# Emitting each engine's instructions straight into the main body instead of inside a Block

## The chip, the cores and the metric

The kernel runs on one core of a Trainium2 chip. The metric is the device time of one execution in microseconds (us). The profile covers a *span*, from the first to the last instruction that it records; the time is 1.3 to 1.9 us longer than the span, and that remainder will matter. Engines are called as in the profile: PE is TensorE (PEld its weight loads), DVE is VectorE, ACT is ScalarE, POOL is GpSimd, SP is SyncE. A "q" after an engine's name means its sequencer.

## The reference

```python
x  = A_x                                   # 1 x 2048 x 512, bf16
xn = layernorm(x)
h[t] = Lam_bar * h[t-1] + (xn @ B_bar.T)[t]           # complex state, 512 wide
A  = 2 * Re(h @ C.T) + xn * Dskip
B  = (gelu(xn @ w_gate) * (xn @ w_up)) @ w_down       # 512 -> 1376 -> 512
out = x + A + B
```

What is computed does not matter here: the change leaves every operation, its order and its waits alone.

## The kernel before

The kernel records its operations, schedules them and then emits one program per engine. An operation waits on semaphores for what it needs and raises one when it is done. The emission is the part that is changed:

```python
        final_waits = [(op.sem, 16) for op in sorted(self.out_ops, key=lambda o: o.finish)]
        block = es.enter_context(nc.Block())

        def body_for(ename):
            prog = plan[ename]

            def body(h):
                for waits, op in prog:
                    for (s, v) in waits:
                        h.wait_ge(s, v)
                    ins = op.fn(h)
                    ins.then_inc(op.sem, 1 if op.kind == "eng" else 16)
                if ename == "sync":
                    for (s, v) in final_waits:      # 17 stores of the output
                        h.wait_ge(s, v)
            return body

        for e in ENGINES:
            if plan[e] or e == "sync":
                {"tensor": block.tensor, "vector": block.vector, "scalar": block.scalar,
                 "gpsimd": block.gpsimd, "sync": block.sync}[e](body_for(e))
```

`nc.Block()` gives each engine a body of its own. In the program that is built from it, the main body ends with one unconditional branch per engine (the entry branch), each engine's body ends with another to the Block's end, and there stands an all-engine barrier: every engine drains (the drain of PE lasts 1.2 us in the records and ends at 174.18 us, 0.05 us after the last matmul) and raises a "gather" semaphore, POOL waits for the other four and raises a "release" semaphore, and every engine waits for that. The records of its line hold the five drains and six semaphore instructions, two of them on POOL and one on each other engine. A barrier of the same form stands at the start of the program (its last records are at 0.66 to 0.72 us), behind POOL's MEMSETs of the constants; it is not part of the Block and stays.

The last lines of the work itself are these. DVE adds the last part of a tile and SP stores it:

```python
                V(lambda e: e.tensor_tensor(OUTB[ko].ap[:, c0:c1], PS[bank][:, c0:c1], XD[tt].ap[:, c0:c1], ALU.add), ...)
                S.dma(lambda e: e.dma_start(out[0, 128 * tt:128 * (tt + 1), c0:c1], OUTB[ko].ap[:, c0:c1]), ...,
                      is_output=True, tag="st_out")
```

Of the kernel before, what the change touches and what calls it, by code (L numbers as in the profile page):

```python
# [77 lines left out]
class Sched:  # L78
# [212 lines left out]
    def emit(self):  # L291
        nc, es = self.nc, self.es
        order = self.order
        esem = {}
        for e in ENGINES:
            if any(op.kind == "eng" for op in order[e]):
                esem[e] = es.enter_context(nc.semaphore("q_" + e))
        cnt = {e: 0 for e in ENGINES}
        nd = 0
        for e in ENGINES:  # L300
            for op in order[e]:
                if op.kind == "eng":
                    cnt[e] += 1
                    op.sem, op.val = esem[e], cnt[e]
                else:
                    op.sem, op.val = es.enter_context(nc.semaphore("d%d" % nd)), 16
                    nd += 1
        self.n_sems = len(esem) + nd
        plan = {}
        nwait = 0  # L310
        for e in ENGINES:
            seen = {}
            prog = []
            for op in order[e]:
                need = {}
                for d in op.deps:
                    if d.kind == "eng" and d.eng == e and (e == "tensor" or d is op.behind):
                        continue
                    key = ("e", d.eng) if d.kind == "eng" else ("d", d.id)
                    if seen.get(key, 0) >= d.val:  # L320
                        continue
                    if key not in need or need[key].val < d.val:
                        need[key] = d
                for key, d in need.items():
                    seen[key] = d.val
                waits = [(d.sem, d.val) for d in need.values()]
                nwait += len(waits)
                prog.append((waits, op))
            plan[e] = prog
        self.n_waits = nwait  # L330
        final_waits = [(op.sem, 16) for op in sorted(self.out_ops, key=lambda o: o.finish)]
        block = es.enter_context(nc.Block())

        def body_for(ename):
            prog = plan[ename]

            def body(h):
                for waits, op in prog:
                    for (s, v) in waits:
                        h.wait_ge(s, v)  # L340
                    ins = op.fn(h)
                    ins.then_inc(op.sem, 1 if op.kind == "eng" else 16)
                if ename == "sync":
                    for (s, v) in final_waits:
                        h.wait_ge(s, v)
            return body

        for e in ENGINES:
            if plan[e] or e == "sync":
                {"tensor": block.tensor, "vector": block.vector, "scalar": block.scalar,  # L350
                 "gpsimd": block.gpsimd, "sync": block.sync}[e](body_for(e))


L, D, P, F = 2048, 512, 512, 1376
# [720 lines left out]
```

## Time and profile before

| | |
|---|---|
| time, median of the first 3 runs | 178.57 us (178.27 to 178.67) |
| profiled execution: time, span | 178.19 us, 176.6 us |
| PE busy | 98% of the span |
| first load and first weight load start | 0.74 and 0.75 us |
| last DVE addition ends, last store is issued | 174.46 and 174.49 us |
| span ends | 176.65 us |

The page of the profile: its first lines, and from its part 4 the chain of work that ended last.

```profile
span 176.6 us, 2515 instructions
## 1 busy us (share of the span) xinstructions
PE 173.4 (98%) x891; PEld 84.9 (48%) x891; DVE 162.4 (92%) x283; ACT 90.3 (51%) x169; POOL 10.3 (6%) x25
...
## 4 chain that ended last, share of the span: by engine, by line
PE 98%; DVE 0%; issue 0%
```

TensorE bounds the body. Nothing that the change removes stands between two matmuls, so only the start and the end can move.

The timeline of the start (start us, duration us, engine, line, operation):

```profile
0.34 0.10 POOL L1060 MEMSET const-uint8-127<- 128x1 uint8 x1
0.74 0.41 SPq L498 DMA_DIRECT2D arena<-in_A_x_dram  x1
0.74 1.28 ACT L480 ACT_TABLE_LOAD   x1 [0.74 <-PEq L1060]
0.75 0.14 PEld L913 LDWEIGHTS PS<-const-bfloat16-1.0 128*128 128x128 bf16 x2 [0.75 <-issue]
```

L1060 is the line that makes the program object; its MEMSETs and the opening barrier carry that number. Between 0.44 us, when the MEMSETs end, and 0.74 us lies the opening barrier, which stays.

The records of the closing barrier's line, L374 (engine, instruction, count: shortest, median, longest in ns, first and last start in us):

```profile
L374 POOLq EVENT_SEMAPHORE  x2: 17/17/17, 176.2 to 176.3; - x2
...
L374 PEldq DRAIN  x1: 1200/1200/1200, 173.0 to 173.0; - x1
...
L374 SPq COMPARE_BRANCH  x1: 33/33/33, 176.0 to 176.0; - x1
L374 SPq DRAIN  x1: 7/7/7, 176.2 to 176.2; - x1
L374 ACTq EVENT_SEMAPHORE  x1: 17/17/17, 176.3 to 176.3; - x1
...
L374 PEldq EVENT_SEMAPHORE  x1: 51/51/51, 176.3 to 176.3; - x1
L374 SPq EVENT_SEMAPHORE  x1: 17/17/17, 176.6 to 176.6; - x1
```

Read it as a chain. SP's branch at 176.0 carries the last of the 17 waits for stores. SP drains and raises the gather; POOL gathers and releases (176.2, 176.3); PE, DVE and ACT pass at 176.3. SP passes last, at 176.6, and with that the span ends. To the nanosecond, from the same records: SP's last paired wait ends at 175.972, its branch stands at 176.038, its drain at 176.177, POOL's release at 176.288, PE's pass at 176.342 and SP's at 176.630.

### The profile page before, as it was taken

Reading aid. Unit: us, or ns where it says so; the run is one execution under the profiler, and the core shown is the slowest. Engines: PE = TensorE matmul, PEld = TensorE weight load, DVE = VectorE, ACT = ScalarE, POOL = GpSimd, SP = SyncE. Lnnn points to the kernel's source line nnn. Section 1 sums busy time; section 2 is a strip of 40 time slices with the busy share of each in tenths; the row PEclk is TensorE's granted clock in tenths of the full one; section 3 lists DMA queues with packets and bytes.
Section 4 is the critical chain, followed back from the end, with each engine's and each line's share of the span. In section 5 each row is a group of like instructions: output and inputs, shape, how many; then the busy total and the mean of one; then the engine's idle time right before and its main releaser. Section 6 shows DMA issues by size and latency. Waiting matters only on the chain.

```text
span 176.6 us, 2515 instructions
## 1 busy us (share of the span) xinstructions
PE 173.4 (98%) x891; PEld 84.9 (48%) x891; DVE 162.4 (92%) x283; ACT 90.3 (51%) x169; POOL 10.3 (6%) x25
## 2 busy tenths in 40 slices
PE   8999999999999999999999999999999999999994
PEld 3954464444544444444644444444454444444453
DVE  6989999987999999889999999999999999999961
ACT  4575568899866898003676792000767780000000
POOL 3212040220000000020000000000000000000000
PEclk9999999999999999999999999999999999999999
DMA  5997999984999000011024000002001000000131
GB/s 156 322 318 162 184 212 158 111 156 89 218 302 185 4 0 2 0 59 59 4 57 92 2 0 0 4 7 82 30 8 21 4 0 0 0 0 0 64 132 46
DMA packets 33396, 14.36 MB, mean 81 GB/s; under 512 B 23688, under 2 KB 33384, under 8 KB 33384
## 3 DMA queue, kind: packets, MB, share of 16 engines
q1 hardware_dynamic: 32944, 13.87, 35.1%
q10 hardware_dynamic: 440, 0.33, 0.6%
q8 instruction: 7, 0.11, 0.3%
q14 instruction: 5, 0.04, 0.1%
HBM read 6.46 MB, written 2.10 MB: 48 GB/s over the span
## 4 chain that ended last, share of the span: by engine, by line
PE 98%; DVE 0%; issue 0%
PE PS L864 37%; PE PS L823 32%; PE PS L734 16%; PE PS L698 7%; PE PS L797 3%; PE PS L913 2%; PE PS L673 1%; PE PS L920 0%; DVE arena L882 0%
## 5 line engine op out<-in xcount | busy, mean ns | idle before, releaser
L864 PE MATMUL PS<-arena 128*128 128x512 bf16 (+3 forms) x323 | 66.2, 367 | 0.0
L823 PE MATMUL PS<-arena 128*128 128x512 bf16 x264 | 58.1, 379 | 0.0
L864 PEld LDWEIGHTS PS<-arena 128*128 128x128 bf16 (+1 forms) x323 | 30.8, 98 | 35.2
L823 PEld LDWEIGHTS PS<-arena 128*128 128x128 bf16 x264 | 25.8, 98 | 30.4
L767 DVE TENSOR_TENSOR_SCAN arena<-arena 128x512 bf16<-128x512 f32 x32 | 38.8, 1253 | 0.0
L838 ACT ACTIVATE arena<-PS 128x512 bf16<-128x512 f32 x33 | 19.8, 599 | 37.0 <-PE PS L823 34.5
L734 PE MATMUL PS<-arena 128*128 128x512 bf16 x128 | 28.1, 379 | 0.0
L842 ACT ACTIVATE arena<-PS 128x512 bf16<-128x512 f32 x33 | 19.7, 597 | 4.7 <-PE PS L823 4.5
L856 ACT ACTIVATE PS<-arena 128x512 f32<-128x512 bf16 (+2 forms) x17 | 9.6, 581 | 20.4 <-PE PS L864 19.7
L734 PEld LDWEIGHTS PS<-arena 128*128 128x128 bf16 x128 | 12.5, 98 | 14.9
L738 ACT ACTIVATE arena<-PS 128x512 bf16<-128x512 f32 x32 | 17.7, 595 | 2.3 <-PE PS L734 2.3
L882 DVE TENSOR_TENSOR arena<-PS,arena 128x512 bf16<-128x512 f32 (+2 forms) x17 | 10.8, 652 | 5.0 <-PE PS L864 4.5
L844 DVE TENSOR_TENSOR arena<-arena 128x512 bf16<-128x512 bf16 x33 | 13.0, 416 | 1.7 <-ACT arena L842 1.4
L698 PE MATMUL PS<-arena 128*128 128x192 bf16 (+2 forms) x80 | 13.1, 320 | 0.0
L624 DVE BATCH_NORM_STATS2 arena<-arena 128x6 f32<-128x512 bf16 x16 | 10.3, 682 | 0.9 <-DMA arena<-in_A_x_dram 0.9
L754 DVE TENSOR_TENSOR arena<-arena 128x4096 bf16<-128x4096 bf16 (+1 forms) x5 | 9.2, 1860 | 0.5 <-ACT arena L619 0.5
L698 PEld LDWEIGHTS PS<-arena 128*128 128x128 bf16 x80 | 7.4, 100 | 4.7 <-issue 0.2
L756 DVE TENSOR_TENSOR arena<-arena 128x4096 bf16<-128x4096 bf16 (+1 forms) x5 | 9.2, 1860 | 0.4 <-ACT arena L620 0.4
L707 ACT ACTIVATE arena<-PS,arena 128x192 bf16<-128x192 f32 (+1 forms) x16 | 6.7, 447 | 4.9 <-PE PS L698 4.1
L779 DVE TENSOR_TENSOR arena<-arena 128x4096 bf16<-128x4096 bf16 x4 | 9.2, 2289 | 0.1
L780 DVE TENSOR_TENSOR arena<-arena 128x4096 bf16<-128x4096 bf16 x4 | 9.1, 2285 | 0.0
L710 DVE SCALAR_TENSOR_TENSOR arena<-PS,arena 128x192 bf16<-128x192 f32 (+1 forms) x16 | 6.6, 444 | 0.7 <-ACT arena L707 0.7
(84 smaller groups left out, 111.1 us busy)
## 6 DMA issues: line engine op xcount, KB each, us to landing
out_dram<-arena SPq DMA_DIRECT2D x15, 128.0 KB, 1.7
arena<-in_A_x_dram SPq DMA_DIRECT2D x3, 512.0 KB, 5.3
arena<-in_B_w_down_dram SPq DMA_DIRECT2D x1, 1280.0 KB, 8.4
arena<-in_B_w_gate_dram SPq DMA_DIRECT2D x2, 256.0 KB, 5.2
arena<-in_B_w_up_dram SPq DMA_DIRECT2D x2, 256.0 KB, 5.4
arena<-in_B_w_gate_dram SPq DMA_DIRECT2D x1, 480.0 KB, 5.8
arena<-in_B_w_up_dram SPq DMA_DIRECT2D x1, 480.0 KB, 5.9
arena<-arena SPq DMA_TRANSPOSE x25, 2.6
```

The lines of the kernel that those rows point to most:

```text
L624: return (V(lambda e: e.bn_stats(ST[tt].ap, X[tt].ap), d_dve_1x(512), [X[tt]], [ST[tt]], "bnst"), V(lambda e: e.bn_aggr(MVt[b][j].ap, ST[t ...
L698: ins_ = e.matmul(dst, XCd(j, k), WGU[:, us[0]:us[-1] + 1, k, f0:f1], start=(k == 0), stop=(k == KD - 1))
L734: ins_ = e.matmul(PS[bank][:, :], BBT[c][dk].ap[:, 128 * s:128 * (s + 1)], XNT[b].ap[:, dk, :], start=(dk == 0), stop=(dk == KD - 1))
L738: GATE["evBu"] = ACT(lambda e, bank=bank, k3=k3, s=s, c=c: e.activation(SSc[k3][s][c].ap, PS[bank][:, :], ACTF.Copy), d_act(512), [BANK[ba ...
L767: V(lambda e, g=g, rb=rb, init=init: e.tensor_tensor_scan(g.ap, rb, g.ap, init, ALU.mult, ALU.add), d_dve_scan(512), [g, PA[RRr]] + ([CARc ...
L823: ins_ = e.matmul(PS[bank][0:m, c0:c1], W.ap[:, dk, 128 * ft:128 * ft + m], XNT[b].ap[:, dk, c0:c1], start=(dk == 0), stop=(dk == KD - 1))
L838: GATE["last_gelu"] = ACT(lambda e, bg=bg, kk=kk, m=m: e.activation(GG[kk].ap[0:m, :], PS[bg][0:m, :], ACTF.Gelu_apprx_tanh), d_act(512), ...
L842: ACT(lambda e, bu=bu, kk=kk, m=m: e.activation(UPB[kk].ap[0:m, :], PS[bu][0:m, :], ACTF.Copy), d_act(512), [BANK[bu]], [UPB[kk]], "evU")
L844: V(lambda e, kk=kk, m=m, ft=ft, k2=k2: e.tensor_tensor(HTt[k2][ft].ap[0:m, :], GG[kk].ap[0:m, :], UPB[kk].ap[0:m, :], ALU.mult), d_dve_tt ...
L856: ACT(lambda e: e.activation(PS[bank][:, c0:c1], X[tt].ap[:, c0:c1], ACTF.Copy), d_act(c1 - c0), [X[tt]], [BANK[bank]], "seed")
L864: ins_ = e.matmul(PS[bank][:, c0:c1], l_[:, 128 * j:128 * (j + 1)], r_[:, c0:c1], start=False, stop=last and n == len(ops) - 1, skip_group ...
L882: V(lambda e: e.tensor_tensor(OUTB[ko].ap[:, c0:c1], PS[bank][:, c0:c1], XD[tt].ap[:, c0:c1], ALU.add), d_dve_1x(c1 - c0), [BANK[bank], XD ...
```

## The change

Its intent is to drop what the Block adds around the work: the entry branch and the closing barrier. The engines' programs are emitted one after the other into the main body; SP still waits for all 17 stores.

```diff
-        block = es.enter_context(nc.Block())
-
-        def body_for(ename):
-            ... (as above)
         for e in ENGINES:
-            if plan[e] or e == "sync":
-                {"tensor": block.tensor, ... "sync": block.sync}[e](body_for(e))
+            h = getattr(nc, e)
+            for waits, op in plan[e]:
+                for (s, v) in waits:
+                    h.wait_ge(s, v)
+                op.fn(h).then_inc(op.sem, 1 if op.kind == "eng" else 16)
+        for (s, v) in final_waits:
+            nc.sync.wait_ge(s, v)
```

## The prediction

> **What bounds the kernel now.** TensorE: the page gives PE 98% busy over a span of 176.6 us at full granted clock, and the chain that ended last is 98% PE. The change touches no PE work, order or wait between operations, so only the two ends of the span can move. The time (178.57 us) is about 1.9 us more than the span; I take that part as constant.

> **The start.** The timeline shows the constants' MEMSETs on POOL (0.24 to 0.44 us), then, after the opening all-engine barrier, SP's first load and PE's first weight load at 0.74 and 0.75 us. That barrier stays. The entry branches have no record: the whole trace holds one branch, SP's at the end (33 ns). So I believe that the entry branch, whose target is the next instruction of its engine, is never executed. [...] on PE only 26 ns lie between the barrier's last record and the first weight load. Gain at the start: 0 to 0.03 us.

> **The end.** The records of the closing barrier's line and of SP's final waits, us from the span's start: SP's last paired wait passed at 175.97; SP's branch, which carries the 17th wait, 176.04 to 176.07; SP's drain 176.18; POOL gathers at 176.21, releases at 176.29; PE, DVE, ACT pass at 176.34; SP last, 176.63 to 176.65, the end of the span. So 0.67 us lie between the last paired wait and the end, all on the critical path. What remains is the 17th wait as an instruction of its own, about 0.07 us after the one before. The span should end at about 176.05: **0.60 us less**. The drains of PE (1.2 us), DVE and ACT go too, but overlap the last store and cost nothing. That store (issued 174.49, seen 175.95) stays.

> **Does the saving reach the time?** [...] SP arrives last before and after, so I expect the whole 0.6 us; a little more if it helps that the others arrive 1 to 2 us earlier[...].

> **Predicted time:** 178.57 - 0.60 - 0.02 = 177.95 us, 0.35% less; 8 in 10: 177.5 to 178.4. The spread before was 0.4 us, so few runs hardly show it. Faster by over 2%: 1%; within 2%: 98%; slower: 1%.

> **What would show each step.** (1) No branch record; five drains, not ten. (2) First load and weight load still at 0.72 to 0.75 us. (3) PE's busy time unchanged to 0.2 us; the last DVE eviction still ends near 174.46. (4) The span ends with SP's waits near 176.05, about 0.1 us after the last store is seen. (5) Time minus span still about 1.9 us.

> **What would make it wrong.** The first ACT table load (1.28 us) could be placed ahead of the opening barrier, since both are now in one body; ACT's drain would hold every engine back by about 0.9 us and the kernel would be 0.3 us slower. I give it 5%: the later two loads stand directly before their activations. [...] Or the time is not counted from the span's end, and the gain is nil.

Where a cut is marked, the passage named a figure or a mechanism that no trace or run of this case shows. None of them was a term of the sum, which stays 178.57 - 0.60 (the end) - 0.02 (the start) = 177.95 us.

## The result, and the profile after

| | before | after |
|---|---|---|
| time, median (range, runs) | 178.47 us (178.27 to 178.68, 6) | 177.87 us (177.40 to 178.10, 6) |
| ratio, 95% interval | | 0.9964 (0.9948 to 0.9979) |
| profiled execution: time, span | 178.19, 176.65 us | 177.82, 176.07 us |
| time minus span, the same execution | 1.54 us | 1.75 us |

The ratio is the mean time of the fast runs of one kernel over that of the other's fast runs of the same rounds, so it is not quite the ratio of the medians. The change is a gain of 0.36%, clear of the noise.

The page after, the same parts, and then the start in its timeline:

```profile
span 176.1 us, 2489 instructions
## 1 busy us (share of the span) xinstructions
PE 172.0 (98%) x876; PEld 84.1 (48%) x891; DVE 162.2 (92%) x283; ACT 90.2 (51%) x169; POOL 10.3 (6%) x25
...
## 4 chain that ended last, share of the span: by engine, by line
PE 94%; DMA 3%; SPq 1%; issue 1%; DVE 0%
```

```profile
0.34 0.10 POOL L1049 MEMSET const-uint8-127<- 128x1 uint8 x1
0.73 1.28 ACT L469 ACT_TABLE_LOAD   x1 [0.73 <-PEq L1049]
0.74 0.40 SPq L487 DMA_DIRECT2D arena<-in_A_x_dram  x1
0.74 0.14 PEld L902 LDWEIGHTS PS<-const-bfloat16-1.0 128*128 128x128 bf16 x2 [0.74 <-issue]
```

15 of PE's 891 matmul records are missing from this trace, so PE's lower busy time means nothing; the 891 weight loads are all there. The 3% of DMA in the chain are the first 7 us, where TensorE's first real matmuls wait 0.3 us for the first weights of B_w_up; in the profile before, PE had no such gap and the chain ran over the warming matmuls instead (matmuls on constants that TensorE runs until the first data are there). The second profile of the same changed kernel, after_again, has no such wait either, so it is scatter and not the change. The start is where it was: without its entry branch SP issues its first load at 0.736 instead of 0.739 us. The ACT table load still stands behind the opening barrier, at 0.73 us.

The barrier's line is gone. The only instructions at the end are SP's waits, line L340:

```profile
L340 SPq EVENT_SEMAPHORE  x9: 17/28/28, 175.0 to 176.0; - x9
```

The last one starts at 176.045 us and the span ends 0.028 us later. The last store was issued at 174.583, a tenth of a microsecond later than in the profile before. That tenth comes from the body: over all executions of the kernel before that ran beside the experiments the span scatters from 176.3 to 177.4 us. So I measure the end of each execution from its own last store:

| us | before | after |
|---|---|---|
| issue of the last store to the end of the span | 2.16 | 1.49 |
| the end of the span to the end of the time | 1.54 | 1.75 |
| sum: issue of the last store to the end of the time | 3.70 | 3.24 |

The first line is the barrier and the branch, 0.67 us. The second line gives 0.2 us of it back, outside of the span. Why it does is what the experiments had to find.

### The profile page after: what moved, and what is told of

It reads as the page before. It is cut to its first block, busy times and chain, and to the rows that moved or that the text cites. A ratio compares the mean times of both kernels' runs of the same rounds, so it can differ in the third digit from the quotient of the medians.

```text
span 176.1 us, 2489 instructions
## 1 busy us (share of the span) xinstructions
PE 172.0 (98%) x876; PEld 84.1 (48%) x891; DVE 162.2 (92%) x283; ACT 90.2 (51%) x169; POOL 10.3 (6%) x25
## 4 chain that ended last, share of the span: by engine, by line
PE 94%; DMA 3%; SPq 1%; issue 1%; DVE 0%
PE PS L853 37%; PE PS L812 32%; PE PS L723 16%; PE PS L687 6%; PE PS L786 3%; DMA arena<-in_B_w_up_dram 3%; SPq L487 0%; PE PS L662 0%; SPq L491 0%; DVE arena L871 0%
## 5 line engine op out<-in xcount | busy, mean ns | idle before, releaser
L812 PE MATMUL PS<-arena 128*128 128x512 bf16 x258 | 57.5, 379 | 0.3
L723 PE MATMUL PS<-arena 128*128 128x512 bf16 x125 | 27.8, 379 | 0.2
```

Of the source, the lines that this page charges most:

```text
L723: ins_ = e.matmul(PS[bank][:, :], BBT[c][dk].ap[:, 128 * s:128 * (s + 1)], XNT[b].ap[:, dk, :], start=(dk == 0), stop=(dk == KD - 1))
L812: ins_ = e.matmul(PS[bank][0:m, c0:c1], W.ap[:, dk, 128 * ft:128 * ft + m], XNT[b].ap[:, dk, c0:c1], start=(dk == 0), stop=(dk == KD - 1))
```

## The experiments

The first theory: the gain is what lay behind SP's last wait, above all the barrier's hops, and the entry branch was never executed. Rivals: the gain comes from the layout of the program (branches, labels, addresses); or from the other engines ending earlier; or it is noise. The first four ran on one chip with 11 runs of the kernel before (median 178.28 us); the next four on a second chip (7 runs, 178.24 us); then three on a third chip (11 runs, 178.39 us); the last on a fourth (11 runs, 178.40 us).

**after_again: the changed kernel once more.** No edit.

> The changed kernel as it is, as the control of this group. Theory (the 0.6 us are the closing barrier's hops behind SP's last wait; the entry branch was never executed): span 176.1 us, time 0.6 us under the kernel before, time minus span 1.7 us as before. Rival 'noise': the difference shrinks under 0.3 us with more rounds.

Measured: 177.78 us, ratio 0.9965 (0.9946 to 0.9984). Noise is out. Last store to end of span 1.495 us, as before. Over all executions of this group time minus span is 1.73 us, against 1.53 us for the kernel before: not "as before". The return of 0.2 us is real.

**one_barrier: one barrier put back, no Block.**

```diff
             nc.sync.wait_ge(s, v)
+        nc.all_engine_barrier()
```

> No Block, but one all-engine barrier put back at the very end: no branch anywhere. Theory: 0.50 to 0.60 us of span come back (176.6), time 178.4, so within 0.15 us of the kernel before. Rival 'layout': the gain comes from leaving the Block (no branches, no labels, other instruction addresses), so the time stays near 177.9 and the barrier costs under 0.2 us.

Measured: 178.24 us, ratio to before 0.9987 (0.9968 to 1.0006); last store to end of span 2.04 us, so 0.55 us of span came back. In time it is 0.39 us over after_again (means 178.15 and 177.76 us), a little less than I had said. The layout theory, which allowed the barrier under 0.2 us, falls. The line of the barrier has the same oddity as in the kernel before: ACT passes at 176.4, SP at 176.7.

```profile
L341 SPq DRAIN  x1: 7/7/7, 176.2 to 176.2; - x1
L341 ACTq EVENT_SEMAPHORE  x1: 17/17/17, 176.4 to 176.4; - x1
...
L341 SPq EVENT_SEMAPHORE  x1: 17/17/17, 176.7 to 176.7; - x1
```

**two_barriers: two of them.** The same line twice.

> No Block, two all-engine barriers at the end. Theory: the second costs about 0.45 to 0.5 us more (drain, gather, release, SP's own pass; in the kernel before 0.47 us from SP's drain to SP's pass), so span 177.1 and time 178.9, above the kernel before. Rival 'layout': no more than 0.2 us above the kernel with one barrier. Rival 'the others must arrive early': all the loss comes with the first barrier, none with the second.

Measured: 178.69 us, ratio 1.0019 (1.0003 to 1.0036). The second barrier added 0.31 us to the part from the last store to the end of the span, not 0.45 to 0.5. In it SP passes first, with the others:

```profile
L342 SPq EVENT_SEMAPHORE  x1: 17/17/17, 176.9 to 176.9; - x1
L342 ACTq EVENT_SEMAPHORE  x1: 17/17/17, 176.9 to 176.9; - x1
```

So a barrier does not make SP late. Something delayed SP in the first one.

**block_no_barrier: the Block kept, its closing barrier emptied.**

```diff
+        def no_closing_barrier():
+            end = nc.main_func.blocks[-1]
+            end.instructions = []
+        es.callback(no_closing_barrier)
         block = es.enter_context(nc.Block())
```

> The Block kept with all its branches and labels, the eleven instructions of its closing barrier taken out. Theory: nearly the whole gain, span 176.1 to 176.2, time 177.9 to 178.0; the one branch left in the trace is SP's, which carries a wait, and costs 0.05 to 0.1 us. Rival 'layout' (entry branch, labels, addresses): time stays at 178.4.

Measured: 177.65 us, ratio 0.9970 (0.9948 to 0.9991), so nearly the whole gain. Last store to end of span 1.585 us: SP's branch, which carries a wait, costs 0.09 us over the changed kernel. All five entry branches are in this program and none is in its trace; its first load starts at 0.735 us.

**all_wait: all engines end together.**

```diff
+        for e in ENGINES:
+            if e != "sync":
+                for (s, v) in final_waits[-1:]:
+                    getattr(nc, e).wait_ge(s, v)
```

> No Block, no closing barrier, but TensorE, VectorE, ScalarE and GpSimd each also wait for the last store, so that all five engines end together. Theory (only SP's hops behind its last wait counted): like the changed kernel, time 0.5 to 0.65 us under the kernel before, time minus span 1.7 us. Rival 'the others arrive early at the runtime's end': part of the gain goes, time minus span grows to 1.9 us or more.

"The runtime's end" is only a name here for what lies between the end of the span and the end of the time, 1.53 us in the kernel before; no record shows what it holds.

Measured: 177.90 us, ratio 0.9975 (0.9952 to 0.9999); time minus span 1.82 us on average. That lies between what the two theories said: more than 1.73, less than 1.9. Where the others end seems to count, a little.

**sem_barrier: a closing barrier without drains.** Why is SP late in the first barrier? Theory A: its drain is slow after its stores. Theory B: it sees its release late.

```diff
+        nc.all_engine_barrier(sem_only=True)
```

> No Block, one closing barrier made of semaphores alone, without drains. From SP's last wait to the end of the span the kernel with one barrier took 0.58 us (176.145 to 176.721). Theory A (SP's drain after its DMA work is slow: SP passed 0.30 us after the other engines in the first barrier, but first in the second): the barrier costs only 0.20 to 0.30 us, and SP passes within 0.05 us of the others. Theory B (SP polls its release late for another reason): SP still passes 0.3 us late, cost 0.45 us or more.

Measured (one execution): SP passes first, at 175.979 us, and the others at 175.984 to 175.991. The barrier costs 0.31 us from the last store to the end of the span. Taken alone, this speaks for A.

**drain_early: a drain of SP in the shadow of the last store.**

```diff
+        nc.sync.drain()
         for (s, v) in final_waits:
             nc.sync.wait_ge(s, v)
+        nc.all_engine_barrier()
```

> No Block, one closing barrier with drains, and one more drain on SP directly behind its last store, while that store is in flight. Theory A: the slow drain is paid there for nothing (SP's final waits start some 0.3 us later, still 0.7 us before the last store is seen), the barrier's own drain is then quick, SP passes with the others and the barrier costs 0.25 to 0.35 us. Theory B: SP still passes 0.3 us after the others, cost 0.55 us.

Measured (one execution, 179.00 us): neither. The early drain took 0.13 us and was over by 175.5 us, long before the last store was seen. SP passed the barrier with the others, at 177.1 us, but its second drain started 0.45 us after the last wait, and the barrier cost 0.78 us instead of 0.55. A falls: the drain was paid for, and the pause came all the same. B falls: SP saw its release at once. The pause had moved from behind SP's drain to before it, and SP had one instruction more than in the kernel with one barrier.

**entry_branch: the entry branch made to execute.** In the trace of before, the one branch with a record is the one that carries a wait. So I gave each entry branch a wait that is met long before.

```diff
+        gone = es.enter_context(nc.semaphore("consts"))
+        go = nc.gpsimd.nop()                 # moved ahead of POOL's drain
+        go.then_inc(gone, 1)
+        for e in ENGINES:
+            getattr(nc, e).wait_ge(gone, 1)
         block = es.enter_context(nc.Block())
```

> The kernel before, with the entry branch of each engine made to execute: it carries a wait that is met long before. Theory (the plain entry branch is never executed): six branch records instead of one, the first load starts 0.05 to 0.15 us later than before (0.79 to 0.89 us), time 178.3 to 178.5. Rival 'the entry branch was executed all along, unrecorded': the first load and weight load start where they did, at 0.74 and 0.75 us, to within 0.02 us.

Measured: 178.89 us, ratio 1.0032 (1.0013 to 1.0052). There are five branch records at the start, 33 ns on POOL, SP and ACT, 47 on DVE and 174 on PE, and one at the end. The first load starts at 0.883 us, 0.14 later, the first weight load at 1.049, 0.30 later (timeline of 0.4 to 1.2 us):

```profile
0.88 0.40 SPq L507 DMA_DIRECT2D arena<-in_A_x_dram  x1
1.05 0.13 PEld L922 LDWEIGHTS PS<-const-bfloat16-1.0 128*128 128x128 bf16 x2 [1.05 <-issue]
```

So the plain entry branch of the kernel before was most likely not executed. The delay is that of a branch with its wait, which this run can't part; that a plain one costs nothing is shown by the start of the kernel after, 0.003 us from the one before. The time rose by more than I had said; again SP had one instruction more, and again its drain at the end came 0.43 us late.

At this point I counted SP's records in every trace. This table is worked out from the records, not printed by the profile: the gap ahead of SP's 80th record, and what that record is.

```
kernel           SP records  gap before the 80th   the 80th record
before                   80              0.446 us   wait for release, closing barrier
one_barrier              80              0.472 us   wait for release, closing barrier
two_barriers             82              0.468 us   wait for release, first barrier
drain_early              81              0.450 us   drain of the closing barrier
entry_branch             81              0.434 us   drain of the closing barrier
sem_barrier              79                     -   (78 in the changed kernel, block_no_barrier, all_wait)
```

**after_pad: eight more instructions on SP, in a part where SP is idle.**

```diff
             for waits, op in plan[e]:
+                if op is first_out:          # SP's first store of the output
+                    waits = [(plan["sync"][0][1].sem, 16)] * 16 + waits
                 for (s, v) in waits:
                     h.wait_ge(s, v)
```

The sixteen waits on the first load are folded two to an instruction: the final waits start eight records later on SP, so that the third of them is the 80th record and not the 72nd. They are long met; VectorE reads what that load brought at 2.9 us in the kernel after.

> The changed kernel with eight extra instructions on SP (waits long met) in a part where SP is idle, so that every later SP instruction stands eight places further on. In all runs so far with at least 80 SP records SP paused 0.43 to 0.47 us before the 80th, whatever it was (drain or wait). Theory C (a pause at a fixed place of SP's instruction stream): the pause now stands before the third of the final waits, hidden behind the last store's flight; last store to end of span stays 1.49 us; time minus span falls from 1.73 us to 1.3 to 1.5, time 177.4 to 177.6, if the changed kernel pays the pause after its span today. Theory A (SP's drain, or the time since the last store, makes the pause): no gap over 0.1 us before the 80th, time minus span stays 1.7, time 177.8.

Measured: 177.32 us, ratio to before 0.9944 (0.9922 to 0.9966). The gap before the 80th record, now the third of the final waits, is 0.442 us, while the last store is in flight. Last store to end of span is 1.50 us, unchanged, and time minus span fell from 1.73 to 1.31 us. Theory C holds in place and in size; the time is 0.08 us under the range that I had given. The kernel is about 0.4 us under the changed one; that compares two ratios to the kernel before, 0.9944 here and 0.9965 in another group, as the two did not run side by side, and their intervals overlap. What carries the claim is time minus span: 1.30 to 1.33 us in all six executions here, 1.67 to 1.77 in all six of after_again, with spans of 175.6 to 176.3 us here and 175.7 to 176.3 there. The line of its final waits shows that they end where they did, at 176.0 us, in spite of the pause among them:

```profile
L343 SPq EVENT_SEMAPHORE  x9: 17/28/28, 174.9 to 176.0; - x9
```

**before_pad: the same eight instructions in the kernel before.**

> The kernel before with the same eight extra SP instructions. Theory C: the pause moves in front of the last store's wait, SP passes the closing barrier with the others, last store to end of span falls from 2.16 to 1.85 us; the time stays within 0.15 us of the kernel before, as time minus the other engines' end was 1.8 us with and without SP being late, so time minus span rises from 1.53 to 1.8. Theory A: SP still passes 0.3 us after the others, nothing changes.

Measured: 178.46 us, ratio 1.0005 (0.9984 to 1.0025). Now SP passes the closing barrier with the others:

```profile
L377 SPq DRAIN  x1: 7/7/7, 175.9 to 175.9; - x1
L377 SPq EVENT_SEMAPHORE  x1: 17/17/17, 176.1 to 176.1; - x1
L377 ACTq EVENT_SEMAPHORE  x1: 17/17/17, 176.1 to 176.1; - x1
```

Last store to end of span fell by 0.24 us to 1.92, the time did not change, and time minus span rose to 1.79 us. In the kernel before SP's lateness cost nothing: the time followed the other engines.

**early_load: the first load ahead of the opening barrier.** The opening barrier is the closing one's sister, and entry_branch had moved the start. So I took the first input load out from behind it, and two of the seven warming matmuls away.

```diff
+        main = nc.main_func.blocks[0]
+        code = list(main.instructions)
+        of = lambda i, kind: str(i.engine).endswith("SP") and kind in type(i).__name__
+        loads = [i for i in code if of(i, "DMACopy")][:1]
+        code = [i for i in code if i not in loads]
+        at = next(n for n, i in enumerate(code) if of(i, "Drain"))
+        main.instructions = code[:at] + loads + code[at:]
-        nwarm = 7
+        nwarm = 5
```

> The changed kernel with the opening barrier taken off the first load: SP issues the first input load ahead of its drain, and TensorE runs 5 instead of 7 warming matmuls. If the start is on the critical path: first load at 0.01 instead of 0.74 us, VectorE's first statistics at 2.1 to 2.3 instead of 2.84 us, time 0.2 to 0.6 us under the changed kernel. If other loads of the start (the second input, the first weights, which stay behind the barrier) bind: no gain over 0.15 us.

Measured: 179.09 us, ratio 1.0040 (1.0009 to 1.0070), a loss. The first statistics came at 2.12 us as hoped. But from its chain that ended last:

```profile
1.06 3.23 DMA arena<-in_A_x_dram
```

and from TensorE's timeline:

```profile
5.57 0.61 PE L669 MATMUL PS<-arena 128*128 128x128 bf16 x4 [1.47 <-DVE arena L936]
```

The second input, issued by ACT at 1.06 us, landed 3.23 us later. SP, one load ahead, had sent its first weights at 0.81 us, in front of it; in the kernel after SP sends them at 1.20, behind it. VectorE's centring of the second tile came at 5.15 instead of 4.13 us and TensorE waited 1.47 us for it. Neither reading of the expectation named this. The six executions fall into two groups, three at 178.50 to 178.60 us and three at 179.58 to 179.70; the profile is of the second, so its long landing explains no more than that one. That the order of the two made it slow is argued here; the next run restores it, with other changes.

**both_early_pad: both inputs ahead of the barrier, with the eight instructions.** The same move for the first load of ACT too, the eight instructions of after_pad, 5 warming matmuls, and ACT's load without its wait on a MEMSET, which it does not need:

```diff
-        S.order_behind(ld_x0(1, "scalar", [wrm]), GATE["table"])
+        ld_x0(1, "scalar")
```

> The changed kernel with the eight extra SP instructions, and with both of the first two input loads (one on SP, one on ACT) issued ahead of the opening barrier, and 5 warming matmuls. In the run with one early load the second input landed 3.2 us after its issue, behind the weights that SP had sent off 0.26 us earlier. Theory (that order made it slow; the start itself is on the critical path): both inputs land at about 2.1 to 2.6 us, TensorE's transposes start at 3.5 to 3.7 instead of 4.25 us, and the time is 0.2 to 0.6 us under the kernel with the extra instructions alone, that is 176.7 to 177.1. Rival (the first 10 us are bound by what the DMA engines bring in, weights included): the transposes start early but a wait for weights or inputs follows, and the time is 177.2 or more.

Measured: 177.38 us, ratio 0.9939 (0.9922 to 0.9957), the same as after_pad at 0.9944. TensorE's timeline shows the transposes at 3.60 us instead of 4.27, and then this wait:

```profile
3.60 0.40 PE L674 MATMUL PS<-arena 128*128 128x128 bf16 x4
...
7.04 0.50 PE L699 MATMUL PS<-arena 128*128 128x192 bf16 x4 [0.40 <-DMA arena<-in_B_w_up_dram]
7.38 0.39 PE L674 MATMUL PS<-arena 128*128 128x128 bf16 x4
7.60 2.48 PE L699 MATMUL PS<-arena 128*128 128x192 bf16 x20
```

VectorE's centring of the second tile came at 3.75 us, so with the old order its input is early again. In the kernel after, the same matmuls start at 7.13 us, after a wait for the same weights. In after_pad, from which this kernel differs only in the start, TensorE does not wait for weights and is at the same place at 7.6 us:

```profile
7.42 0.39 PE L665 MATMUL PS<-arena 128*128 128x128 bf16 x4
7.64 2.48 PE L690 MATMUL PS<-arena 128*128 128x192 bf16 x20
```

Of the 0.65 us by which the transposes start earlier, 0.04 are left. The rival holds: by 7 us waits for the weights, 0.35 us for B_w_gate and 0.40 for B_w_up, have eaten the early start. For the two inputs, the opening barrier is off the critical path as long as the weights come no sooner.

## Why the prediction was right

The time was 177.87 us against 177.95 forecast. The saving at the end of the span was right in its mechanism; that the number came so close is in part luck, as two errors, named below, had opposite signs. The steps:

- *The start: 0 to 0.03 us.* Right. The first load moved by 0.003 us. block_no_barrier shows the Block's entry branches present and leaving no record, with the first load at 0.735 us, and entry_branch shows them with a wait on them: five records of 33 to 174 ns, and the first load 0.14 us later.
- *The end: 0.60 us of span.* The mechanism was right, the term too small: the end of the span came 0.67 us nearer to the last store. I had reserved 0.07 us for the 17th wait as an instruction of its own at the very end. In the program it stands alone at the front of the nine instead, where it costs nothing, and the last two waits share one instruction.
- *The parts of it.* By block_no_barrier SP's exit branch is worth 0.09 us, by one_barrier the barrier 0.55 us, of the span.
- *Does the saving reach the time? "I expect the whole 0.6 us."* This step was wrong: it took "0.67 us, all on the critical path" because SP arrives last, and took time minus span as constant. Its error was offset in part by the one before. Time minus span did not stay constant but grew by 0.2 us. (The prediction's 1.9 us for it set the median of other runs against the profiled span; within one execution it was 1.54.) From the last store to the end of the time it went from 3.70 to 3.24 us, so by this measure 0.46 us of the 0.67 reached the time. The mean times beside each other in the first group are 178.34 and 177.76 us, 0.58 apart; the 0.12 us between I put down to the body's scatter, which is not shown (the same excess, worked out the same way, is -0.06 us in before_pad, 0.04 in one_barrier and 0.15 in block_no_barrier), and 0.46 us lies inside the interval of the ratio (0.2 to 0.5% of 178.5 us, that is 0.4 to 0.9 us).
- *The ACT table load ahead of the barrier.* Did not happen: it starts at 0.73 us. The 0.9 us was an estimate, which the profile before allows: 1.28 us of load put ahead of ACT's opening drain (it starts at 0.14 us) would end that drain 0.9 us after POOL's, which ends at 0.49.

What the runs show in place of the failed step is a rule for the end, which all 14 profiled executions follow to within 0.04 us. The time ends at the later of two: 1.80 us after the last of PE, DVE, ACT and POOL has ended, or after SP has ended 1.31 us if SP's pause lies inside its stream and 1.75 if it is yet to come. Eleven of them, worked out from the records; "others" is the end of those four, "SP" is SP's end, both in the span of that execution, "time" its time:

```
kernel            others     SP     time   the later of the two
before            176.39  176.65  178.19   others + 1.80
one_barrier       176.44  176.72  178.24   others + 1.80
before_pad        176.13  176.09  177.92   others + 1.79
two_barriers      176.96  176.91  178.74   others + 1.78
entry_branch      177.13  177.09  178.93   others + 1.80
all_wait          176.37  176.34  178.17   others + 1.80
after             174.56  176.07  177.82   SP + 1.75
block_no_barrier  174.10  175.71  177.48   SP + 1.77
early_load        176.29  177.81  179.58   SP + 1.77
after_pad         174.50  176.02  177.33   SP + 1.31
both_early_pad    174.46  175.97  177.32   SP + 1.34
```

The constants were fitted on these same executions. What was forecast before it ran is what the pads did: that after_pad would take the pause off the remainder, and that before_pad would shorten the span and not the time. In every execution in which the others set the time PE was the last of them (by 0.03 us), so the runs do not tell whether all four count or PE alone.

Before, the barrier made the other four wait for the stores, and they set the time. SP passed 0.25 us after the last of them had ended (176.65 and 176.39), because of its pause, and that had cost nothing. So the change took 0.67 us off the span of which only 0.42 were on the path. After, SP alone sets the end, and its remainder with the pause is 1.75 us instead of the others' 1.80, 0.05 less: 0.42 + 0.05 is the 0.46 us measured, but for rounding. The pause, 0.44 us by the two constants for SP (1.75 and 1.31), was in the shadow of nothing any more, and invisible, as it came after the span. It also explains why one instruction more on SP made drain_early and entry_branch lose some 0.4 to 0.5 us at the end: the pause (0.450 and 0.434 us) came to stand before SP's drain, where it held up all five engines, which pass at 177.1 us in both.

What is the pause? The runs do not show it. The DMA records of the trace show what goes together with it: one packet of 8192 bytes, of the kind that the page lists as "instruction", follows the end of the pause by 0.57 to 0.94 us in all eight kernels that have it in the span, and where the eight extra instructions moved the pause forward by more than a microsecond, the packet moved with it (from 177.26 us in the kernel before to 175.77 in before_pad, from 177.21 in the changed kernel to 176.06 in after_pad). In the executions whose SP stream ends before its 80th instruction, the packet comes 1.10 to 1.17 us after SP's end (1.42 in early_load), where a pause yet to come would put it. The records do not name the engine that a packet is for. Nor do the runs exclude that the recording makes the pause: its place is counted in recorded instructions, and every execution was recorded. That the packet follows the pause and does not end it is what the records show; what SP waits for in it stays open. Open is also why the four other engines have 0.49 us more behind them than SP: no record lies there.

## What to carry to other kernels

Removing this Block's closing barrier saved what stood behind the last wait, 0.67 us of span and about 0.5 us of time. The plain entry branches to the next instruction left no record and cost no time here (first load at 0.739 us with them, 0.736 without), so look for a record before counting one. Measure the end of a kernel from its last store to the end of the time, not to the end of the span: what lies after the span depended here on which engine ended last (1.80 us after the last of PE, DVE, ACT and POOL, 1.31 or 1.75 after SP). If the engine that waits for the outputs pauses at a fixed place of its stream, as SP did here for 0.43 to 0.47 us before its 80th record, see whether a few instructions where it is idle move the pause into a wait that exists anyway; here that was worth another 0.4 us (177.32 us with it moved, 177.78 without, on two chips), nearly as much as the change itself, in executions that were all recorded.
